# An mLSTM and Fourier-mixing kernel: its 64-row products cut into 64x64 tiles, and a one-column product widened to 128 columns

## The chip, the cores and the metric

The kernel runs on one core of one Trainium2 chip. Its time is the device time of one execution in microseconds (us), from start to end; less is better. A profile is one execution taken by the hardware profiler. It knows the engines PE (TensorE, matrix products), DVE (VectorE), ACT (ScalarE), POOL (GpSimd) and SP (which issues the DMAs here).

## The reference, cut to what matters

Two parts follow each other. The first is an mLSTM cell on q, k, v of shape (4 batches, 8 heads, 768 tokens, 40 features) with an input, a forget and an output gate. Step by step over the tokens it keeps a 40x40 state C and a vector n per head:

```
C = f * C + i * outer(v_t, k_t)      n = f * n + i * k_t
y_t = sigmoid(o_t) * (C q_t) / max(|n . q_t|, 1)      (f, i stabilised by a running maximum m)
```

The heads are joined to x of shape (4, 768, 320). The second part is a Fourier-mixing block:

```
u = x + real(fft(fft(x, axis=1), axis=2))
un = (u - mean(u)) / sqrt(var(u) + 1e-6)
out = u + relu(un @ w_ch1) @ w_ch2           (w_ch1 320x1280, w_ch2 1280x320)
```

All of it is in float32 (the two weight matrices come as float64 and are converted on the chip).

## The kernel before, in words

The mLSTM is worked in chunks of 128 tokens. In the first batch a chunk is a full 128x128 block of scores for each head (`mlstm_scores`, L591); in the three later batches it is two blocks of 64x64 (`halves_scores`, L678). Heads are packed in pairs: heads 0 to 3 lie on SBUF partitions 0 to 39, heads 4 to 7 on partitions 64 to 103, so one head's product has 40 rows and sits in the upper or lower half of the PE array. `product` (L580) is the helper that issues one matmul, and most of the small ones carry its line, L581. The pattern `TILES` (L653) runs through the four combinations of a row half and a column half of the array, in this order: (0,0), (1,1), (0,1), (1,0).

The Fourier transform along the tokens is a product with a table (`mix_products`, `mix_products_again`), and the one along the features is `mix_feat` (L961): for each of three groups of 128 frequencies, three matmuls into one PSUM bank `pu`. The 385th frequency (index `LAST` = 384) is left over. In the middle group two more matmuls have that one column of Z and Zt as the stationary operand and write one row of PSUM, `own`. `mix_add` (L983) reads that row.

The first matrix of the MLP has 320 input features: 128, 64 and 128. Full 128x128 matmuls (L1122, L1185) work the two blocks of 128 (in the later batches with a scheme that needs seven products for eight, whose sums DVE makes at L1194). The 64 features between are the "rest": `w1_rest(n)` holds 64 rows for an even block of hidden features on partitions 0 to 63 and 64 rows for the odd block on partitions 64 to 127. For these, two matmuls of 64 rows and 128 columns follow each other, one in the upper and one in the lower half of the array, each into its own PSUM bank of 128 hidden features by 384 tokens. In the first batch that is `between` (L1110, matmul at L1113), ten times; in each later batch it is `tails` (L1187, matmul at L1190), twice in step 2 of each of the five calls of `mlp_block`. There the order on PE is: a full product into bank p1, `tails(1)` into p3 and p5, `tails(0)` into p2 and p1, and in step 3 `begin(i + 1)`, a full product into the bank that p3 had. The matmul into p5 waits for a DVE sum (L1194), the one into p1 for an ACT copy (L1226), and `begin` for the DVE sum that reads p3. The second matrix (L1258 in the first batch, L1314 in the others) uses full tiles.

The order on each engine is written out by hand: `at(slot, phase, ...)` puts each function in a slot and `run` issues them slot by slot, so that pieces of one batch's mLSTM stand between pieces of the batch before's MLP. The four phases EVAC, FILL, MAIN and FILL_PE order the pieces within a slot. Every engine works its own list in that order and waits on semaphores.

A float32 matmul of the program shows in the trace as two weight loads (engine PEld) and two matmuls (engine PE), which I call its two passes; counts below are of these.

Of the kernel before, what the change touches and what calls it, by code (L numbers as in the profile page):

```python
# [19 lines left out]
L = 128  # L20
# [6 lines left out]
DM = H * D  # L27
DFF = 4 * DM
NFF = DFF // L
TAIL = DM - 2 * L  # L30
# [6 lines left out]
NC = HALF_D + 1  # L37
COL = (0, L, 2 * L)
LAST = 3 * L
# [18 lines left out]
def kernel(  # L58
# [15 lines left out]
    nc = tc.nc  # L74
# [15 lines left out]
    first_heads_ps = ps_early.enter_context(tc.tile_pool(name="ps_h", bufs=1, space=PSUM)).tile([L, 2, 4 * L], FP, name="hb")  # L90
# [3 lines left out]
    def bank(name, shape, n=None):  # L94

        return ps_m.tile(shape, FP, name=name, tag=f"pm{next(turn) if n is None else n}")
# [9 lines left out]
    dd_sb = const.tile([L, 4, DM + 1], FP, name="dd_sb")  # L106
# [20 lines left out]
    def at(slot, phase, fn, *args):  # L127
        plan.setdefault((slot, phase), []).append((fn, args))
# [16 lines left out]
    def gates(gp):  # L145
# [138 lines left out]
        pt = columns(first, 1)  # L284
        spread_max(0, 0, NP)
        mlstm_scores(0, 0)
        sums(others)
        mlstm_exp(0, 0, 0)
# [210 lines left out]
    def w1_block(ch, f):  # L499
        return w1_sb[:, f // 2, (2 * ch + f % 2) * L:(2 * ch + f % 2 + 1) * L]  # L500

    def w1_rest(n):
        return w1_sb[:, n, 4 * L:]
# [87 lines left out]
    def mlstm_scores(b, c):  # L591

        k = chunks[b, c]
        k.ps = [ps_s.tile([L, NP, L], FP, name=f"ps{hip}", tag="ps") for hip in range(2)]
        for p in range(NP):
            for hip in range(2):
                r = slice(hip * 64, hip * 64 + D)
                nc.tensor.matmul(k.ps[hip][:, p, :], k.qk[r, 1, p, :], k.qk[r, 0, p, :], start=True, stop=True)  # L598

    def mlstm_weigh(b, c):  # L600
        k = chunks[b, c]
# [49 lines left out]
    banks = {}  # L651

    TILES = ((0, 0), (1, 1), (0, 1), (1, 0))  # L653
# [8 lines left out]
    def half(n):  # L662
        return slice(n * LH, (n + 1) * LH)
# [297 lines left out]
    def mix_feat(b, p, part=slice(None)):  # L961

        k = mixes[b]
        m = slice(COL[p], COL[p] + L)
        if part.start in (None, 0):
            k.pu[p] = bank("pu", [L, DM + 1 + NC], MIX[b - 1]["u"][p] if b > 0 else None)
        pu = k.pu[p]  # L970
        if b == 0:
            products = ((pu[:, 0:DM + 1], k.Z[:, 0, m], dd_sb[:, 0]), (pu[:, 0:DM + 1], k.Z[:, 1, m], dd_sb[:, 1]),
                        (pu[:, 0:DM + 1], k.Zt[:, m], dd_sb[:, 2]))
        else:
            products = ((pu[:, 0:NC], k.Z[:, 0, m], dd_sb[:, 0, 0:NC]), (pu[:, NC:DM], k.Z[:, 1, m], dd_sb[:, 1, 1:HALF_D]),
                        (pu[:, 0:DM], k.Zt[:, m], dd_sb[:, 3, 0:DM]))
        if p == TG - 2:
            last, own = slice(LAST, LAST + 1), first_heads_ps[0:1, 1, 0:NC] if b == 0 else pu[0:1, DM + 1:]
            products += ((own, k.Z[:, 0, last], dd_sb[:, 0, 0:NC]), (own, k.Zt[:, last], dd_sb[:, 3, 0:NC]))
        for i, (o, z, t) in list(enumerate(products))[part]:  # L980
            nc.tensor.matmul(o, z, t, start=(i == 0 or b == 0 and i == 3), stop=(i in (2, 4)), skip_group_check=True)  # L981

# [74 lines left out]
    def plan_mix(b, s0, x_done, s_feat, s_add, s_turn):  # L1057
# [20 lines left out]
        for p in range(TG):  # L1078
            for i in range(3) if b == 0 and p == TG - 1 else ():
                at(s_feat[p] + i, FILL_PE + 5.1, mix_feat, b, p, slice(i, i + 1))  # L1080
            if b == 0 and p == TG - 2:
                at(s_feat[p], FILL_PE + 4.06, mix_feat, b, p, slice(0, 3))
                at(s_feat[p] + 3, FILL_PE + 5.05, mix_feat, b, p, slice(3, 5))
            elif b == 0 and p == 0:
                at(s_feat[p], FILL_PE + 4, mix_feat, b, p, slice(0, 2))
                at(s_feat[p], FILL_PE + 4.04, mix_feat, b, p, slice(2, 3))
            elif b > 0 or p < TG - 1:
                at(s_feat[p], FILL_PE + 4, mix_feat, b, p)
# [10 lines left out]
                at(t + 1, EVAC, mix_turn_out, b, c)  # L1099


    IN_ORDER = ((0, 0), (0, 1), (1, 0), (1, 1), (0, 2), (1, 2), (0, 3), (1, 3), (0, 4), (1, 4))

    def mlp_in(b, gr, f):


        k = mixes[b]
        u = [uT_bufs[gr][:, ch].rearrange("p c t -> p (c t)") for ch in range(3)]

        def between(pm, n, u, start):  # L1110
            for i in range(2):
                r = slice(i * TAIL, (i + 1) * TAIL)
                nc.tensor.matmul(pm[i], w1_rest(n)[r], u[r], start=start, stop=not start,  # L1113
                                 skip_group_check=True)


        n = IN_ORDER.index((gr, f // 2))
        ahead = n > 3 and n % 2 == 1
        if f % 2 == 0:
            k.pm = k.pm_next if ahead else [bank("pm", [L, TG * L]) for _ in range(2)]  # L1120
        for i, ch in ((1, 1),) if f % 2 else ((0, 0), (0, 1), (1, 0)):
            nc.tensor.matmul(k.pm[i], w1_block(ch, f // 2 * 2 + i), u[2 * ch], start=(ch == 0 and not ahead),  # L1122
                             stop=(ch == 1 and ahead), skip_group_check=True)
        if f % 2 and not ahead:
            between(k.pm, f // 2, u[1], False)
            if n > 3:
                k.pm_next = [bank("pm", [L, TG * L]) for _ in range(2)]
                gr, i = IN_ORDER[n + 1]
                between(k.pm_next, i, uT_bufs[gr][:, 1].rearrange("p c t -> p (c t)"), True)
# [4 lines left out]
    def hidden(gr, f):  # L1134
        return hid[gr, f % 2][:, f // 2 * TG * L:(f // 2 + 1) * TG * L]
# [7 lines left out]
    def block(t, n):  # L1143
        return t[:, n * L:(n + 1) * L]
# [20 lines left out]
    def mlp_u(gr, ch):  # L1165
        return uT_bufs[gr][:, ch].rearrange("p c t -> p (c t)")
# [8 lines left out]
    def mlp_block(b, i, step):  # L1175

        k = mixes[b]
        f = 2 * i  # L1180
        T2, T3, T4 = w1x["T"]
        A = {(r, ch): w1_block(ch, f + r) for r in range(2) for ch in range(2)}

        def product(bank, w, u, start=False):
            nc.tensor.matmul(bank, w, u, start=start, stop=True, skip_group_check=True)  # L1185

        def tails(gr, banks):  # L1187
            for r, bank in enumerate(banks):
                rows = slice(r * TAIL, (r + 1) * TAIL)
                nc.tensor.matmul(bank, w1_rest(i)[rows], mlp_u(gr, 1)[rows], start=False, stop=True,  # L1190
                                 skip_group_check=True)

        def add(h, bank):
            nc.vector.tensor_tensor(out=h, in0=h, in1=bank, op=OP.add)  # L1194

        banks = list(range(4) if i % 2 else range(3, -1, -1))

        def begin(i):


            k.p1 = bank("pm", [L, TG * L], 0 if i % 2 else 3)
            product(k.p1, w1_block(0, 2 * i), mlp_u(0, 0), True)
            nc.scalar.copy(out=hidden(0, 2 * i), in_=k.p1)

        (h11, h21), (h12, h22) = ([hidden(gr, f + r) for r in range(2)] for gr in range(2))
        if step == 0:
            if i == 0:
                begin(0)
            k.pm = [k.p1, bank("pm", [L, TG * L], banks[1])]
            product(k.pm[1], A[0, 1], mlp_u(0, 2), True)  # L1210
        elif step == 1:
            k.pm.append(bank("pm", [L, TG * L], banks[2]))
            p1, _, p5 = k.pm
            if i == 0:
                product(p5, A[1, 0], mlp_u(1, 0), True)
            product(p1, block(w1x["S2"], i), T2)
            nc.scalar.copy(out=h12, in_=p1)
            if i > 0:
                product(p5, A[1, 0], mlp_u(1, 0), True)
            add(h12, p5)  # L1220
        elif step == 2:
            k.pm.append(bank("pm", [L, TG * L], banks[3]))
            p1, p2, p5, p3 = k.pm
            product(p3, block(w1x["S4"], i), mlp_u(1, 2), True)
            product(p1, block(w1x["S3"], i), T3)
            nc.scalar.copy(out=h22, in_=p1)  # L1226
            tails(1, (p3, p5))
            tails(0, (p2, p1))
            add(h12, p3)
            add(h22, p5)  # L1230
            add(h11, p2)
        else:
            p1 = k.p1
            if i < NFF // 2 - 1:
                begin(i + 1)
            product(p1, A[1, 1], T4)
            nc.scalar.activation(out=h21, in_=p1, func=AF.Relu, scale=-1.0)
# [107 lines left out]
    def plan_mlp(b, s):  # L1345
        groups = range(NT // TG)
        for i in range(NFF // 2) if b > 0 else ():
# [4 lines left out]
            for n, (gr, f) in enumerate(((1, 2 * i + 1), (1, 2 * i), (0, 2 * i))):  # L1352
                at(*((s - 1, MAIN + (-0.1 if gr else 0.1)) if end else (s + n, MAIN + 0.5)), mlp_relu_in_place, gr, f)
        for gr, n in IN_ORDER if b == 0 else ():
            for f in (2 * n, 2 * n + 1):
# [248 lines left out]
```

## Time and profile before

| what | value |
|---|---|
| time, median of 3 runs | 397.08 us (395.04 to 399.1) |
| span of the profiled execution | 392.9 us |
| median of the runs over that span | 4.2 us |
| PE busy | 379.7 us, 97% of the span, 4342 matmuls |
| DVE, ACT, POOL busy | 281.2, 174.6, 134.9 us |
| granted PE clock | 1.000 |
| matmuls in tiles of 64 rows by 128 columns, busy | L1190 26.3 us (120), L1113 8.3 us (40), L598 7.0 us (96) |
| matmuls with one stationary column (L981), busy | 2.6 and 0.8 us (12 and 4) |

The profile gives the execution's span, from its first to its last instruction. Its own time with what lies around the span is not recorded; the median of the runs stands 4.2 us above it. Busy times of PE are not the work of the array: matmuls are pipelined and overlap, so the distance from one start to the next tells more than a duration. Rows written 64*128 mean 64 rows and 128 columns of the array in use; after that stand the partitions by elements of the moving operand.

### The profile page before, as it was taken

How to read it: one execution, taken by the hardware profiler on the slowest of the kernel's cores; microseconds unless marked ns; L12 is line 12 of the kernel's file. 1: busy time of each engine (PE TensorE's matmuls, PEld its weight loads, DVE VectorE, ACT ScalarE, POOL GpSimd, SP SyncE). 2: the span in 40 equal slices, each digit the busy share in tenths (PEclk: the TensorE clock that was granted, in tenths of full speed). 3: DMA queues.
4: the chain of work that ended last, by engine and by line, in shares of the span. 5: the costliest groups of instructions: out<-in, count | busy, mean ns of one | idle time of the engine just before them, and what ended most of it. 6: DMA issues, size and time to landing. Idle time of an engine off the chain costs nothing.

```text
span 392.9 us, 10881 instructions
## 1 busy us (share of the span) xinstructions
PE 379.7 (97%) x4342; PEld 277.5 (71%) x4342; DVE 281.2 (72%) x668; ACT 174.6 (44%) x505; POOL 134.9 (34%) x238
## 2 busy tenths in 40 slices
PE   8999888999999999999999998999999999999996
PEld 6888454556577767665478898666588996556996
DVE  7788898798897286787964796876855785346651
ACT  5978766757442133654443043654530033444000
POOL 5665434775595132561421424560300000020000
DMA  7869499697981343464002633710000001000000
GB/s 227 287 191 305 135 235 262 176 274 214 248 208 35 94 129 119 135 178 126 0 1 64 180 99 92 215 35 3 0 2 33 3 33 35 0 0 2 34 35 33
DMA packets 21614, 43.96 MB, mean 112 GB/s; under 512 B 3492, under 2 KB 9852, under 8 KB 21436
## 3 DMA queue, kind: packets, MB, share of 16 engines
q1 hardware_dynamic: 21564, 43.27, 37.5%
q8 instruction: 34, 0.56, 0.6%
q14 instruction: 16, 0.13, 0.1%
HBM read 39.16 MB, written 4.10 MB: 110 GB/s over the span
## 4 chain that ended last, share of the span: by engine, by line
PE 80%; DVE 11%; ACT 2%; issue 2%; DVEq 0%; ACTq 0%
PE po L1314 21%; PE pm L1185 16%; PE po L1258 8%; PE pm L1122 7%; PE pm L1190 6%; PE ph L581 5%; PE ps L581 4%; PE pu L981 3%; PE pz L936 2%; PE pm L1113 2%; PE hb L581 1%; PE put L1028 1%; PE pzt L936 1%; DVE so L771 1%; PE ps L598 1%
## 5 line engine op out<-in xcount | busy, mean ns | idle before, releaser
L1264 DVE SCALAR_TENSOR_TENSOR x<-po,rstd,x 128x160 f32<-128x160 f32 (+1 forms) x69 | 27.2, 394 | 38.8 <-PE po L1314 36.3
L1194 DVE TENSOR_TENSOR h<-h,pm 128x384 f32<-128x384 f32 x60 | 30.5, 548 | 26.8 <-PE pm L1190 12.4
L577 POOL TENSOR_SCALAR_AFFINE_SELECT W<-W 64x512 f32<-64x512 f32 x36 | 28.4, 790 | 32.5 <-ACT W L550 31.3
L704 POOL TENSOR_TENSOR C<-C,decB 128x164 f32<-128x164 f32 x33 | 19.1, 578 | 58.6 <-DVE C L711 52.5
L1185 PE MATMUL pm<-uT,w_sb 128*128 128x384 f32 x90 | 37.8, 507 | 0.2 <-DVE uT L1173 0.2
L550 ACT ACTIVATE W<-W,colT 128x64 f32<-128x64 f32 x144 | 36.6, 336 | 0.0
L1258 PE MATMUL po<-w_sb,h 128*128 128x320 f32 x120 | 34.1, 435 | 0.0
L1052 POOL TENSOR_TENSOR t<-rstd 128x6 f32<-128x6 f32 x12 | 3.7, 310 | 80.2 <-DVE v L1046 79.6
L562 POOL TENSOR_TENSOR qg<-qk,Gb 128x512 f32<-128x512 f32 x21 | 27.3, 1298 | 10.6 <-PE put L1028 10.3
L1122 PE MATMUL pm<-uT,w_sb 128*128 128x384 f32 x80 | 29.3, 499 | 0.7 <-issue 0.7
L1314 PE MATMUL po<-T,S 128*128 128x160 f32 x180 | 28.0, 302 | 1.1 <-DVE x L1264 1.1
L1258 PEld LDWEIGHTS po<-w_sb,h 128*128 128x128 f32 x120 | 22.3, 190 | 9.1 <-issue 0.6
L1314 PEld LDWEIGHTS po<-T,S 128*128 128x128 f32 x180 | 25.4, 190 | 2.7 <-DVE x L1264 1.3
L1190 PE MATMUL pm<-uT,w_sb 64*128 64x384 f32 x120 | 26.3, 511 | 0.3 <-DVE h L1194 0.3
L1314 PE MATMUL po<-w_sb,h 128*128 128x160 f32 x180 | 26.3, 300 | 0.0
L1314 PEld LDWEIGHTS po<-w_sb,h 128*128 128x128 f32 x180 | 25.2, 190 | 1.5 <-DVE x L1264 0.3
L1185 PEld LDWEIGHTS pm<-uT,w_sb 128*128 128x128 f32 x90 | 15.4, 189 | 13.9 <-DVE h L1194 5.9
L1241 ACT ACTIVATE h<-h 128x384 f32<-128x384 f32 x45 | 23.1, 519 | 3.0 <-DVE h L1194 3.0
L1017 ACT ACTIVATE uc<-x 128x384 f32<-128x384 f32 x24 | 14.4, 613 | 19.9 <-DVE x L1009 19.9
L1190 PEld LDWEIGHTS pm<-uT,w_sb 64*128 64x128 f32 x120 | 12.7, 185 | 12.8 <-issue 8.2
L1033 ACT COPY uT<-put 128x384 f32<-128x384 f32 x21 | 9.6, 477 | 26.9 <-PE put L1028 26.8
L1122 PEld LDWEIGHTS pm<-uT,w_sb 128*128 128x128 f32 x80 | 14.1, 189 | 10.4 <-issue 3.2
(259 smaller groups left out, 848.0 us busy)
## 6 DMA issues: line engine op xcount, KB each, us to landing
kvt<-in_kv SPq DMA_DIRECT2D x24, 336.0 KB
qk<-in_qkT SPq DMA_DIRECT2D x48, 160.0 KB
raw<-in_w SPq DMA_DIRECT2D x10, 640.0 KB
Gb<-G_d SPq DMA_DIRECT2D x42, 128.0 KB
W<-M_d SPq DMA_DIRECT2D x36, 128.0 KB
so<-in_o SPq DMA_DIRECT2D x24, 160.0 KB
out<-x SPq DMA_DIRECT2D x24, 160.0 KB
ds_sb<-in_dft_s SPq DMA_DIRECT2D x1, 1158.0 KB
```

The costliest lines, as they stand in the source:

```text
L550: nc.scalar.activation(out=k.W[:, h, :], in_=M, func=AF.Exp, scale=-1.0, bias=colT[:, c, 0, b * H + h:b * H + h + 1])
L562: nc.gpsimd.tensor_tensor(out=k.qg[:, :, t], in0=k.qk[:, 0, :, t], in1=k.Gb[:, :, t], op=OP.mult)
L577: nc.gpsimd.affine_select(out=W, in_=W, compare_op=OP.is_ge, fill=0.0, base=base, pattern=[[0, H], [-1 if back else 1, LH]], channel_multi ...
L581: nc.tensor.matmul(out, w, x, start=start, stop=True, skip_group_check=True)
L1122: nc.tensor.matmul(k.pm[i], w1_block(ch, f // 2 * 2 + i), u[2 * ch], start=(ch == 0 and not ahead), stop=(ch == 1 and ahead), skip_group_c ...
L1185: nc.tensor.matmul(bank, w, u, start=start, stop=True, skip_group_check=True)
L1190: nc.tensor.matmul(bank, w1_rest(i)[rows], mlp_u(gr, 1)[rows], start=False, stop=True, skip_group_check=True)
L1194: nc.vector.tensor_tensor(out=h, in0=h, in1=bank, op=OP.add)
L1241: nc.scalar.activation(out=h, in_=h, func=AF.Relu, scale=-1.0)
L1258: nc.tensor.matmul(k.po[m], hidden(gr, f)[:, i * L:(i + 1) * L], w2_sb[:, f, :], start=(f == 0), stop=(f == NFF - 1))
L1264: nc.vector.scalar_tensor_tensor(out=u, in0=po, scalar=k.rstd[:, c:c + 1], in1=u, op0=OP.mult, op1=OP.add)
L1314: nc.tensor.matmul(po, a[:, f], w[:, f], start=start and f == 0, stop=f == half - 1, skip_group_check=True)
```

## The change

Three places change, all in the order and form of matmuls; no other engine's instructions do.

1. `rest_products` takes the place of the two matmuls of `between` and of `tails`. Each matmul of 64 rows by 128 columns becomes two of 64 by 64 (column half 0, then column half 1), so a pair becomes four: upper and lower half for the first 64 hidden features, then upper and lower half for the other 64. The moving operand, 384 tokens, is the same for both column halves.
2. `mlstm_scores` of the first batch does the same with its 40 rows by 128 columns: each matmul becomes two with 64 keys, in the order of `TILES`.
3. In `mix_feat` the stationary column of the last frequency is repeated 128 times (a broadcast view, no copy), and `own` is 128 equal rows of PSUM in place of one. `mix_add` still reads row 0.

```
-            for hip in range(2):
+            for hip, i in TILES:
                 r = slice(hip * 64, hip * 64 + D)
-                nc.tensor.matmul(k.ps[hip][:, p, :], k.qk[r, 1, p, :], k.qk[r, 0, p, :], start=True, stop=True)
+                product(k.ps[hip][half(i), p, :], k.qk[r, 1, p, half(i)], k.qk[r, 0, p, :], True)
...
-            last, own = slice(LAST, LAST + 1), first_heads_ps[0:1, 1, 0:NC] if b == 0 else pu[0:1, DM + 1:]
-            products += ((own, k.Z[:, 0, last], dd_sb[:, 0, 0:NC]), (own, k.Zt[:, last], dd_sb[:, 3, 0:NC]))
+            own = first_heads_ps[:, 1, 0:NC] if b == 0 else pu[:, DM + 1:]
+            z, zt = (t[:, LAST:LAST + 1].to_broadcast([L, L]) for t in (k.Z[:, 0], k.Zt))
+            products += ((own, z, dd_sb[:, 0, 0:NC]), (own, zt, dd_sb[:, 3, 0:NC]))
...
+    def rest_products(banks, n, u, start):
+        for cols in range(2):
+            for i in range(2):
+                nc.tensor.matmul(banks[i][half(cols)], w1_rest(n)[half(i), half(cols)], u[half(i)], start=start,
+                                 stop=not start, skip_group_check=True)
...
         def between(pm, n, u, start):
-            for i in range(2):
-                r = slice(i * TAIL, (i + 1) * TAIL)
-                nc.tensor.matmul(pm[i], w1_rest(n)[r], u[r], start=start, stop=not start,
-                                 skip_group_check=True)
+            rest_products(pm, n, u, start)
...
         def tails(gr, banks):
-            for r, bank in enumerate(banks):
-                rows = slice(r * TAIL, (r + 1) * TAIL)
-                nc.tensor.matmul(bank, w1_rest(i)[rows], mlp_u(gr, 1)[rows], start=False, stop=True,
-                                 skip_group_check=True)
+            rest_products(banks, i, mlp_u(gr, 1), False)
```

## The prediction

> **What bounds the kernel now.** I read the page's busy times and chain first, then the chain of waits in order of time, window by window, then the timeline around single groups.
>
> ```profile
> PE 379.7 (97%) x4342; PEld 277.5 (71%) x4342; DVE 281.2 (72%) x668; ACT 174.6 (44%) x505; POOL 134.9 (34%) x238
> ...
> PE 80%; DVE 11%; ACT 2%; issue 2%; DVEq 0%; ACTq 0%
> ```
>
> PE is the bound, but not everywhere: the chain lies on DVE and ACT from 31.3 to 61.6 us and at 170.6 to 181.1, 227.9 to 237.1 and 266.3 to 269.0. Time saved on PE counts where the chain is on PE, or where DVE was itself waiting for PE. In the chain of waits (start, duration, what, count) three stretches hold the prices:
>
> ```profile
> 19.38 0.60 PE hb L581 x16
> 19.98 1.09 PE ps L598 x16
> 21.07 1.02 PE hb L581 x16
> ...
> 87.95 0.61 PE ph L581 x32
> 88.55 0.80 PE ps L581 x64
> 89.36 0.47 PE ph L581 x32
> 89.82 3.42 PE pm L1122 x10
> 93.25 1.49 PE pm L1113 x8
> 94.73 0.61 PE ph L581 x32
> ...
> 136.79 1.28 PE pu L981 x6
> 138.07 2.69 PE po L1258 x10
> 140.76 1.72 PE pu L981 x10
> 142.48 2.89 PE po L1258 x10
> ```
>
> What is to be seen: a group costs more when the group before it had another tile shape. 32 matmuls in 64x64 tiles take 0.61 us after a change of shape and 0.47 later within one shape: 0.14 for the change. Fourteen full matmuls at L1185 take 4.71 us (194.46 in the same chain), ten at L1122 take 3.42, so one is (4.71 - 3.42) / 4 = 0.32, and 4.71 - 14 x 0.32 leaves 0.20 for the change. The eight of L1113 run two at a time: four steps of 0.32 are 1.29, and 0.20 is left again. **So the change of shape costs 0.20 us into 128 columns and 0.14 into 64.** The first load cannot be fetched ahead there; L1190's loads take 185 ns on average and those of L581's `ps<-qk` 134, which gives the same 0.05.
>
> **The MLP's rest, part by part.** A pair of 64x128 matmuls already fills the array. Four 64x64 tiles do the same work in the same two steps of 0.32 us, so "four at a time" saves nothing in the steps. It saves at the edges: 0.05 at each entry from full tiles, and the whole entry of 0.14 where L581's 64x64 work stands right behind (94.73 above), as no change of shape is left. The exit to full tiles stays at 0.20. Where these lie in the chain:
> - First batch: seven entries, three of them followed by L581 (63.7, 78.3, 94.7): 7 x 0.05 + 3 x 0.14 = 0.77. All on PE's chain.
> - Second batch, five blocks: 165.3, 185.5 and 199.2 give 0.05 each, 0.15. Those at 174.3 (with L581 behind it) and 191.7 give nothing, below.
> - Third: 253.8, 262.9, 273.4 and 286.2 give 0.20, and L581 behind the second 0.14; 279.6 nothing: 0.34.
> - Fourth: five of 0.05, 0.25. Here each block is 1.49 and 4.78 with nothing else in it, so this stage shows the price most purely.
>
> ```profile
> 174.72 0.66 DVE fe L874
> ...
> 177.18 0.65 DVE h L1194 x2
> ...
> 191.78 0.49 ACT h L1226
> 192.27 0.03 issue
> 192.30 0.56 DVE h L1194
> 192.86 0.04 issue
> 192.90 1.55 PE pm L1190 x6
> ```
>
> At 174 DVE works through its own list (181.1 is when PE gets its next release), so an earlier PE gains nothing. At 191.7 and 279.6 the matmul into p5 waits for DVE's sum. There the new order has a price: the second column halves of p3 and p5 stand behind that wait, where before p3 ran ahead alone. p3 is then done with p5, two steps (0.64) later than now, and DVE's sum of p3 (0.55), which `begin` needs, ends about as late as PE's last tile. I take the 0.05 for lost and the bound at -0.1 each. The wait of p1 for ACT's copy (166.67) holds up p2's second half the same way, but both are wanted only after p1, and ACT was released by PE.
>
> **The last frequency.** The six matmuls of a group take 1.28 - 0.20 = 1.08 us without the entry. In 140.76 the same six and four more take 1.72: 0.64 for the four. They stream 161 columns like two of the six, 0.134 each, 0.54, so 0.10 is the change into one column; the 2.89 behind it against the usual 2.69 is the change back, 0.20. With 128 columns both go and the load of 190 ns lies beside the matmul before. 0.30 a batch; at 142, 222 and 308 it counts (0.90), at 57 it doesn't: DVE is at its own work until 59.0.
>
> **The first batch's scores.** From 1.09 us: the 64x64 group ahead of it takes 0.60 for 16, minus 0.14 is 0.11 to 0.12 for four matmuls of 128 columns. Eight such steps are 0.9, with no entry since shape and neighbour agree: 0.19 less. Chunks 2, 3 and 4 lie on the chain, 0.57; the other three save 0.05 off it. Behind them the chain goes through ACT (31.33 on) and DVE, fed by DMAs with a busy share of 0.76 before 31 us. Nothing shows what comes next there: bounds 0 and 0.57; I take 0.40, since ACT and DVE are released by PE at the seam.
>
> **Waits added.** As built, the new program holds 23 waits of PE on its own earlier matmuls, on a bank that 64x64 tiles wrote last. The nearest target is 38 matmuls back, microseconds earlier, so the wait itself is over. Seven are instructions of their own on PE's list; such ones take 51 ns today, beside running matmuls. 0, at most 7 x 0.05 = 0.35. All other engines keep order and waits; SP's and POOL's queues are passed by nothing. PE's list grows by 256 matmuls and 256 loads. PE once stops for 0.73 us at 81.82 with no cause shown; if that is the list's supply, it may move: 0.7 either way.
>
> **Sum.** 0.77 + 0.15 + 0.34 + 0.25 + 0.90 + 0.40 = 2.8 us: the span goes from 392.9 to 390.1. With the 4.2 around it, or from the median of 397.08, **394.3 us**, 0.7% less. The runs shown differ by 1%, so within 1% is about what a measurement here can't tell from no change.
>
> **Rivals.**
> - *Everything counts* (0.14). With the edges that I gave up, 0.57 - 0.40, 0.30 at 57, 0.14 and 3 x 0.05 in the DVE stretches, it is 3.6 us: 393.5. For it: DVE partly waits for PE even there.
> - *Others take over* (0.12). If DVE, ACT and DMAs hold the old pace up to 269 us, only 308, 286 and the fourth batch are left and one block of the third, 0.65: 396.4. For it: DVE's stretches above; against: each begins at a release by PE.
> - *Loads of one row half exclude its matmuls* (0.08). Two column tiles now share each row half. If the load for the second pass had to wait for matmuls in the same half, each step after a set's first would show its load: 45 steps in L1190 and 13 in L1113, 58 x 0.05 = 2.9, which eats the gain: 397.2; with whole loads of 134 ns 58 x 0.13 = 7.5, 401.8. Against it, the 64x64 groups of today load while they run:
>
> ```profile
> 24.06 0.51 PE L581 MATMUL hb<-qg,C 40*64 40x128 f32 x12
> ...
> 24.07 0.26 PEld L581 LDWEIGHTS hb<-qg,C 40*64 40x64 f32 x8
> ```
>
> [...]
> - *Slower: the four tiles don't stream together* (0.04). If one row half can feed only one column half its 384 moving columns at a time, each of 40 sets takes 0.64 more, 25.7, and 48 score steps 0.11 more: about 425. It decides from the first set, at 62.8 us. Against it: 16 matmuls of 128 columns in 0.60. For it: those have 40 rows, not 64, and the two column tiles read different columns.
>
> **How the numbers follow.** The forecast has 0.62. The range goes from the full gain, less some 1.2 for the spread of the runs, 392.2, to the mild case of the third rival, 397.2. Faster by over 1% (below 393.1): half of the first rival and a fifth of the forecast, by the spread, 0.20. Slower by over 1%: the last rival and the dear end of the third, 0.07. Within 1%: 0.73.
>
> **What will show it.** In the fourth batch 1.49 should become 1.44 beside an unchanged 4.78; ten matmuls at L981 about 1.6 and the next group 2.69; L581 behind the rest 0.47 in place of 0.61; scores 0.9. A set near 2.7 would mean the last rival, 1.6 or more the third. I am wrong if these come and the end doesn't move: then DVE or DMAs took it.

## The result and the profile after

The changed kernel takes 393.95 us (median of 20 runs, 391.01 to 397.99), the kernel before 396.47 us on the same chip (20 runs, 394.55 to 401.45). The ratio is 0.994 with a 95% interval of 0.991 to 0.997: 2.4 us less, where 2.8 were forecast. The span of the profiled execution went from 392.9 to 391.3 us. Executions more than 1.5% above the fastest of their kernel are left out of all ratios, though not of the medians; the profile of one experiment below (part 1 alone) is such an execution, so only its pause and its clock are read from it.

The page of the changed kernel: busy times, the queue that brings instructions (packets, MB, share), and the shares of the chain.

```profile
PE 378.4 (97%) x4598; PEld 275.4 (70%) x4598; DVE 282.4 (72%) x668; ACT 175.3 (45%) x505; POOL 134.1 (34%) x238
...
q8 instruction: 36, 0.59, 0.6%
...
PE 83%; DVE 8%; issue 2%; ACT 1%; DMA 1%; POOL 0%; SPq 0%; DVEq 0%; ACTq 0%
```

PE has 256 matmuls more and 1.3 us less of busy time. Its instructions come in 36 packets instead of 34; that is taken up below.

The chain of waits of the changed kernel (start, duration, what, count), at the places that the prediction named:

```profile
19.91 0.60 PE hb L581 x16
20.51 0.87 PE ps L581 x32
...
89.22 3.42 PE pm L1128 x10
92.65 1.45 PE pm L1108 x16
94.10 0.45 PE ph L581 x32
...
139.91 1.63 PE pu L982 x10
141.54 2.69 PE po L1261 x10
...
192.13 1.51 PE pm L1108 x14
...
193.65 4.78 PE pm L1191 x14
...
219.72 1.63 PE pu L982 x10
221.35 5.66 PE po L1317 x40
...
331.42 1.45 PE pm L1108 x16
332.87 0.01 issue
332.88 4.78 PE pm L1191 x14
```

Nearly every price came as forecast. Scores take 0.87 us (forecast 0.9, before 1.09). A set of the first batch takes 1.45 (1.49 before), and the L581 group behind it 0.45 in place of 0.61: its change of shape is gone. Ten matmuls of the last frequency take 1.63 (1.72 before), and the group behind them 2.69 (2.89). In the third batch, though, the group behind is 5.66 us, where it was 5.64 with the change of shape in it: there the exit's 0.20 came back as something else. And in the block at 192.13 the loss that the prediction described is there: 1.51 and 4.78, together as long as before.

### The profile page after: what moved, and what is told of

The parts are those of the page before. It is cut to its first block, busy times and chain, and to the rows that moved or that the text cites. A ratio compares the mean times of both kernels' runs of the same rounds, so it can differ in the third digit from the quotient of the medians.

```text
span 391.3 us, 11400 instructions
## 1 busy us (share of the span) xinstructions
PE 378.4 (97%) x4598; PEld 275.4 (70%) x4598; DVE 282.4 (72%) x668; ACT 175.3 (45%) x505; POOL 134.1 (34%) x238
## 4 chain that ended last, share of the span: by engine, by line
PE 83%; DVE 8%; issue 2%; ACT 1%; DMA 1%; POOL 0%; SPq 0%; DVEq 0%; ACTq 0%
PE po L1317 21%; PE pm L1191 17%; PE po L1261 8%; PE pm L1108 8%; PE pm L1128 7%; PE ph L581 5%; PE ps L581 4%; PE pu L982 3%; PE pz L936 2%; PE hb L581 1%; PE put L1029 1%; PE pzt L936 1%; PE pz L948 1%; DVE so L771 1%; DVE stats L1009 1%
## 5 line engine op out<-in xcount | busy, mean ns | idle before, releaser
L550 ACT ACTIVATE W<-W,colT 128x64 f32<-128x64 f32 x144 | 36.8, 338 | 0.0
L1108 PE MATMUL pm<-uT,w_sb 64*64 64x384 f32 x320 | 34.1, 498 | 0.4 <-DVE h L1197 0.4
L1191 PEld LDWEIGHTS pm<-uT,w_sb 128*128 128x128 f32 x90 | 15.4, 189 | 14.7 <-DVE h L1197 6.7
L1108 PEld LDWEIGHTS pm<-uT,w_sb 64*64 64x64 f32 x320 | 11.5, 131 | 20.3 <-issue 16.2
L568 POOL TENSOR_TENSOR vw<-kvt,colT 128x328 f32<-128x328 f32 x23 | 20.1, 875 | 4.8 <-DVE colT L289 2.5
```

Of the source, the lines that this page charges most:

```text
L550: nc.scalar.activation(out=k.W[:, h, :], in_=M, func=AF.Exp, scale=-1.0, bias=colT[:, c, 0, b * H + h:b * H + h + 1])
L1108: nc.tensor.matmul(banks[i][half(cols)], w1_rest(n)[half(i), half(cols)], u[half(i)], start=start, stop=not start, skip_group_check=True)
```

## The experiments

### Each part alone

Part 1 alone has the new `rest_products` and the old scores and last frequency; part 3 alone and part 2 alone are the other two hunks of the diff. Parts 1 and 3 ran on one chip, part 2 on another.

> Only the MLP's rest in 64x64 tiles; scores and last frequency as before. My theory (the gain lies at the edges of a set, where the tile shape changes): in the fourth batch a set takes 1.45 us in place of 1.49 and a block 6.25 in place of 6.27; behind a set in the first batch L581 takes 0.14 less; L981's ten matmuls stay at 1.72 and the group behind them at 2.89. Span from the first 128x128 transposes of the chain (L1028, near 62 us) to the end: 0.8 to 1.2 us shorter, ratio 0.997. Rival (the gain that the changed kernel showed between 62 and 110 us is the pause of 0.73 us at 81.8 that happened not to come): the stretch from there to the first products at L1258 is shorter by under 0.3 us wherever the pause is there, and the ratio is 1.000.

> Only the last frequency's stationary column repeated to 128; the rest as before. My theory: the ten matmuls at L981 take 1.63 us in place of 1.72 and the group behind them 0.20 less, in each of the three later batches, 0.29 each; what of it is left at the end depends on who waits next. In the changed kernel 0.38 was lost again at 151 us and 0.2 at 224; if DVE's own pace takes it, both losses come again here (0.3 to 0.5 us left of 0.87, ratio 0.999). Rival (the loss at 151 us is a pause that comes by chance): nothing is lost at 151, only at 224; 0.6 to 0.7 us left, ratio 0.998.

> Part 2 alone: only the first batch's scores are cut into 64x64 tiles. The predicted theory: each of the six groups of scores goes from 1.09 to about 0.87 us, and 0.40 of the 0.57 us of the groups on the chain reach the end: ratio 0.999. Rival: ACT, DVE and the DMAs take the whole of it back before 62 us (in the changed kernel the chain at 62 us was already 0.42 us late): the first product into the MLP's first bank starts at 61.6 us or later, and the ratio is 1.000. Both lie inside the interval of the times, so the trace decides: 61.2 us for that start by the first theory, 61.6 or later by the second.

| kernel | median us (runs) | kernel before, same chip | ratio, 95% interval |
|---|---|---|---|
| part 1, rest | 393.25 (13) | 394.97 | 0.9938 (0.9909 to 0.9968) |
| part 2, scores | 394.38 (12) | 396.39 | 0.9946 (0.9911 to 0.9982) |
| part 3, last frequency | 396.07 (12) | 394.97 | 1.000 (0.9975 to 1.0026) |

The three gains do not add up: 0.6 and 0.5 and 0 per cent make 1.1, and together they are 0.6; with intervals of about 0.3 each side this alone could be noise. But they go against the traces too. Part 3 shows its 0.30 at 140.5 and 305.6 us in its own trace, as forecast, and none of it in the time. Here the granted clock of PE, which is recorded for every execution, matters: ten of part 3's twelve executions had a mean clock below 0.998. The two at full clock have a median of 393.63 us, against 394.62 for the fourteen such executions of the kernel before. For part 1 it is 393.00 (5), for part 2 393.05 (2) against 395.04 (11). "Why PE pauses" returns to this. Part 2 shows nothing in the trace that could be 2 us. Its chain in the first batch:

```profile
19.69 0.87 PE ps L581 x32
...
28.55 2.70 DMA so<-in_o
31.25 1.27 POOL qg L562
32.57 1.69 PE hb L581 x32
...
41.33 1.92 PE pz L948 x4
...
47.39 1.50 PE pz L948 x4
```

The scores are 0.22 us shorter, but then the chain leaves PE for a DMA that lands at 31.25 and POOL's work on it, where it was on PE and ACT before. The first group of the MLP (L1028) starts at 61.36 us against 61.63, and the whole stretch was already 0.28 us early at 17 us, ahead of any edited group. So in this trace nothing of the scores' gain reaches the MLP, as the second theory of that expectation says. But the two traces did not have the same clock. Here it is halved from 41.9 to 45.3 us, and PE is on the chain there (four matmuls at L948 take 1.92 us, four later ones 1.50); in the trace of before it is not. From the start of the pG group ahead of them to the MLP's first group (L1028 here), the five traces with the old scores and no such dip before 62 us take 43.98 to 44.41 us, the two with the new scores 43.80 and 44.56. What the scores are worth at the end stays open. What else differs between this trace and the one of before is a pause of PE: 0.73 us at 81.82 us before, gone here. It is taken up below.

### Two more changes of shape in each block

To price the edges in the fourth batch, the product with T4 is moved between the two `tails` of a block, in the old and in the new form. Each block then has two sets apart, so one more entry and one more exit.

```
             tails(1, (p3, p5))
+            product(p1, A[1, 1], T4)
             tails(0, (p2, p1))
...
-            product(p1, A[1, 1], T4)
             nc.scalar.activation(out=h21, in_=p1, func=AF.Relu, scale=-1.0)
```

> The kernel before, with one change: in mlp_block the last full product into p1 stands between the two sets (upper and lower halves of the second group, then of the first), so that each of the 15 blocks has one change of tile shape more in each direction; all matmuls are the same. My theory: 0.20 into 64x128 and 0.20 out of it, 0.40 a block, less the 0.06 that the next block's first product now waits for DVE's sum: 6.27 becomes 6.61 in the fourth batch; in all 13 to 15 blocks 4.5 to 5.5 us longer, ratio 1.012 to 1.014. Rival (the edges cost nothing of their own, the matmuls' distance is set by something else): a block stays at 6.27, ratio 1.000.

> The changed kernel with the same reordering as the split of the kernel before. My theory: an extra entry into 64x64 costs 0.14 to 0.15 and the exit 0.20, 0.35 a block less the 0.06 of DVE's wait: 6.25 becomes 6.53 in the fourth batch; 3.5 to 4.5 us longer than the changed kernel, that is 1.5 to 2 us longer than before, ratio to before 1.004 to 1.006, and 0.05 a block less than the other split. Rival (a set of 64x64 tiles has another gain than its entry): the distance between the two splits is that between the unsplit kernels, 0.025 a block and not twice the entry's 0.05.

Measured: 404.39 us, ratio 1.0216 (1.0163 to 1.027), with the old tiles, and 401.39 us, 1.0138 (1.0091 to 1.0185), with the new ones. The chain of waits in the fourth batch, first with 64x128 tiles, then with 64x64:

```profile
338.93 0.84 PE pm L1190 x4
339.77 0.84 PE pm L1185 x2
340.61 0.84 PE pm L1190 x4
341.46 4.26 PE pm L1185 x12
```

```profile
338.14 0.81 PE pm L1108 x8
338.94 0.84 PE pm L1191 x2
339.79 0.81 PE pm L1108 x8
340.59 4.26 PE pm L1191 x12
```

Two steps of 0.32 are 0.645, so an entry or an exit costs 0.195 each with 128 columns, and the new entry is 0.03 to 0.04 cheaper, near the 0.05 of the prediction. The block went from 6.27 to 6.79 us, though, 0.52 and not 0.34 more; fifteen blocks of 0.52 are 7.8 of the 9.4 us by which the first median lies above the kernel before, where 4.5 to 5.5 were expected. The 4.26 us hold 12 x 0.3225 = 3.87, the exit's 0.195, and 0.195 that are new. The timeline of the first kernel shows them:

```profile
342.34 0.48 ACT L1203 COPY h<-pm 128x384 f32<-128x384 f32 x1 [2.90 <-PE pm L1185]
...
342.87 0.30 PEld L1185 LDWEIGHTS pm<-raw 128*128 128x128 f32 x2 [0.54 <-ACT h L1203]
```

With the T4 product gone from between, only two matmuls cover ACT's copy of p1, and the next product into p1 waits for it: 0.09 us of wait, and 0.10 because the load of the waiting matmul is no longer beside another's stream (both begin at 342.87 us). The two moved matmuls had hidden that.

Old and new tiles are 0.08 us apart in these blocks (6.79 and 6.71), but only 0.02 in the blocks as they are (6.27 and 6.25). The timeline of one set of the changed kernel tells why:

```profile
331.35 1.52 PE L1108 MATMUL pm<-uT,w_sb 64*64 64x384 f32 x16
...
331.72 0.47 PEld L1108 LDWEIGHTS pm<-uT,w_sb 64*64 64x64 f32 x8 [0.17 <-issue]
332.27 1.48 DVE L1197 TENSOR_TENSOR h<-h,pm 128x384 f32<-128x384 f32 x3 [1.23 <-PE pm L1108]
332.88 0.30 PEld L1191 LDWEIGHTS pm<-uT,w_sb 128*128 128x128 f32 x2 [0.68 <-DVE h L1197]
```

`begin`, the first full product behind the set, waits for DVE's sum of p3, which ends 0.055 us before it starts: also in the kernel before, and in every block of this stage. The time from the set's first matmul to `begin` is set by p3's end and DVE's 0.555 us, not by the exit, so of 0.04 saved about half is left. In the split blocks the second set's exit is followed by a product that no sum holds up.

The same lines decide the rival of the exclusive loads. The loads for the later passes run from 331.72 on beside matmuls in the same two row halves, and the steps behind a set's first stay at 0.32 us, so none of them shows a load.

### The order of rows and columns

```
-        for cols in range(2):
-            for i in range(2):
+        for i in range(2):
+            for cols in range(2):
```

> The changed kernel with the two loops of the rest exchanged: both column halves of the upper row half, then both of the lower. Theory: at 191.7 and 279.6 us the second column half of p3 stood behind the wait of p5 for DVE's sum, and begin for DVE's sum of p3. With p3 complete ahead of the wait, that sum starts about 0.5 us earlier, begin is held by PE alone, and each of the two blocks gains 0.05 to 0.15 us; the blocks without a late sum change by less than 0.03. Together 0.1 to 0.3 us, below what the times can show. Rival: begin is held there by the four tiles themselves, and the two blocks stay at 1.51 us.

In the block at 191.7 the set itself stays at 1.51 us, but there and in the one at 279.6 the full products behind it take 4.71 in place of 4.78: `begin` no longer waits for DVE, since p3 is complete before the matmul that waits. That is 0.07 us a block, within the expected 0.05 to 0.15. The time of the one execution (396.07 us, span 394.4) says nothing on that. PE's granted clock was halved for about 3 us, and here it fell on the chain; in the windows of PE, PEld, DVE, ACT and POOL the clock is the third number from the end:

```profile
66.00:68.00 2.00, 2.00 (x70) 1.92 (x63) 1.82 (x2) 0.65 (x2) 1.94 (x2) 0.50 1.02 317
```

The changed kernel's own profile has such a dip too (its mean clock is 0.996), at 40.8 to 44.2 us. PE is on its chain there: four matmuls at L948 take 2.16 us at 42.62, and 1.50 at 47.94.

### Putting 64x64 groups side by side

If the gain is the change of shape, more of it is to be had by letting more groups of the mLSTM stand right behind a set. For the third and fourth batch's mLSTM the stride of its slots is four, as that of the MLP's blocks, in place of three. The slots of `mix_fold_again` and of what follows the mLSTM move with it.

```
-            at(s + 3, MAIN - 0.1 if end else FILL_PE, halves_from_state, b, c)
+            at(s + stride, MAIN - 0.1 if early_end else FILL_PE, halves_from_state, b, c)
...
-            plan_halves(b, s_mlstm)
+            plan_halves(b, s_mlstm, 3 if b == 1 else 4)
...
-    plan_batch(2, 54, 83, s_mlp + 2 * MLP_SLOTS)
-    plan_batch(3, 86, 115, s_mlp + 3 * MLP_SLOTS)
+    plan_batch(2, 53, 83, s_mlp + 2 * MLP_SLOTS)
+    plan_batch(3, 85, 115, s_mlp + 3 * MLP_SLOTS)
```

> The changed kernel with the mLSTM of the third and the fourth batch put on a stride of four slots in place of three, so that each of its groups of 64x64 products stands right behind a set of the rest. If the price of a change of tile shape (0.14 us into 64 columns, 0.20 back) is what the change saves, four isolated groups in each of two batches lose their pair of changes: 8 x 0.34 = 2.7 us less than the changed kernel, a ratio of about 0.987 to the kernel before. Rival: the order of DVE's work decides there (the chain lies on DVE at 171 to 181 and 258 to 269 us), and the moved mLSTM brings its sums late at other places: ratio 0.994 as the changed kernel, or worse.

> The kernel before with the same new order. The groups stand behind a set there too, but the set has 64x128 tiles, so a change into 64 columns (0.14 us) stays at each: 8 x 0.34 - 8 x 0.14 less what the one neighbour in each batch paid already, 1.9 us less than the kernel before, a ratio of 0.995; the distance to the same order with 64x64 tiles should be about 3.2 us, where it was 2.4 in the old order. Rival: if the order acts through DVE alone, both orders have the same distance of 2.4 us.

Slower, both: 401.72 us with the new tiles, ratio 1.0101 (1.0058 to 1.0144), and 400.24 with the old ones, 1.0127 (1.0056 to 1.0198). The chain of the first shows the gain and what ate it:

```profile
163.20 1.45 PE pm L1109 x16
164.65 0.45 PE ph L581 x32
...
168.28 0.52 ACT h L1245
168.79 1.91 ACT W L550 x8
170.70 0.37 ACT h L1221
```

The group behind the set costs 0.45, without its change. But ACT's eight exponentials of the next chunk (L550, 1.91 us) now stand ahead of ACT's copy of p1 (L1221) in the same slot, and the next product into p1 waits for that copy: PE works on other products meanwhile and stands idle for the last 0.68 us before 171.11. That happens in two blocks of each of the two batches, 2.7 us of idle time in all. Three more waits are for DVE's `uT` (L1180), 2.7 us with 1.9 the longest; the changed kernel has one, of 0.2. The old tiles in the new order have the same waits. So the rival held, with ACT beside DVE.

Whether the tiles still make a difference in this order the medians can't tell, as the clocks differ. In the new tiles' trace it is halved from 251.9 to 255.3 us, and six products there take 3.87 us where the other trace, at full clock, has 2.37:

```profile
251.77 3.87 PE pm L1192 x6
```

```profile
253.60 2.37 PE pm L1186 x6
```

The executions at full clock have medians of 397.69 us with the new tiles (2) and 400.14 with the old (3). That is 2.45 less: nearer to the rival's 2.4 than to the 3.2 expected, from very few executions.

### Why PE pauses

A pause of PE that the chain calls "issue" had been left open by the prediction. The traces of the first ten kernels held eight pauses of over 0.9 us (from one start on PE to the next) with no wait that the profile shows. They have one thing in common. If the matmuls, weight loads and stand-alone waits of PE are counted from the beginning of the trace, PE stops at entry 193 + 256 n and nowhere else. A packet of the instruction queue brings about as many, as an estimate from the kernel before: 34 packets of 16 KB for 8770 entries, 258 each.

| kernel | pause, us | ends at, us | entry | = 193 + 256 x | from the start of packet n to the end of the pause, us |
|---|---|---|---|---|---|
| before | 1.22 | 82.55 | 1985 | 7 | 2.76 |
| part 3 alone | 1.13 | 82.28 | 1985 | 7 | 2.51 |
| split, old tiles | 1.31 | 83.28 | 1985 | 7 | 2.61 |
| new order, old tiles | 1.49 | 82.74 | 1985 | 7 | 2.94 |
| split, new tiles | 1.68 | 86.34 | 2241 | 8 | 2.84 |
| part 1 alone | 1.98 | 179.39 | 5057 | 19 | 2.54 |
| new order, new tiles | 0.95 | 185.94 | 5313 | 20 | 2.48 |
| new order, new tiles | 1.92 | 260.46 | 7105 | 27 | 2.61 |
| changed kernel (a smaller one) | 0.52 | 150.97 | 4289 | 16 | 2.72 |

About 0.32 of each is the normal step. I read this as PE running out of instructions: the packet with its next 256 has begun to move, and PE goes on 2.5 to 2.9 us after that. A group of the mLSTM (32, 64 and 32 matmuls with as many loads in 1.9 us) uses up a whole packet in less time than that, and where PE stopped, a mark had fallen into or just behind such a group. The packets begin about when PE enters the packet before (between 5.1 us ahead and 4.4 us behind in all traces, 0.9 behind in the middle). PE ran dry with one packet outstanding: in the kernel before that packet began at 79.79 us, PE went on at 82.55, and the next packet began only at 84.41.

Marks move with the number of entries ahead of them. That is a thing to test: small matmuls without any use, put where PE waits for ACT (60.3 to 61.6 us), move all marks behind. They also keep PE busy where it had waited.

```
             pt = k.pt[c] = banks["heads"][:, n % 2, 0:3 * L].rearrange("p (ch t) -> p ch t", ch=3)
+            for m in range(10 if n == TG else 0):
+                i, j = TILES[m % 4]
+                product(banks["heads"][half(j), i ^ j, 4 * L - 4:4 * L], ident[half(i), half(i)], ident[half(i), 0:4], True)
```

Each such matmul is four entries; 10, 28, 10 and 24 of them are used.

> The kernel before with ten small extra matmuls (40 entries of PE's list, 64x64 tiles, four columns) put where PE waits for ACT at 60.3 to 61.6 us; their result is read by nobody. Theory of the list: PE's instructions come in packets of 256 (16 KB, 34 of them), PE stops at entry 193 + 256 n of its list if it gets there less than about 2.6 us after packet n began to move, and a packet begins about 0.6 us (quiet DMAs) to 1.4 us (busy) after PE passed entry 193 + 256 (n - 1). Forty entries more move these marks into the dense 64x64 groups: pauses of about 2.0 us (1.0 to 2.6) near 80.2 us and 2.0 us near 149.5 us in place of the 0.9 us at 81.8: 3.2 us longer (2.2 to 4.4), ratio 1.008. Rival: the pauses have another cause, and the extra matmuls fall into PE's idle time: ratio 1.000, the pause where it was.

> The same with 28 extra matmuls (112 entries). Theory of the list: the marks fall into full-tile work nearly everywhere, the pause at 81.8 goes and none comes in its place: 0.8 us shorter, less at most 0.3 us for the extra matmuls if they do not fit into PE's idle time, ratio 0.998. Rival: as the kernel before, the pause at 81.8 stays, or all is longer by the extra matmuls. The trace decides, as the times show 0.8 us hardly.

> The changed kernel with ten extra matmuls (40 entries) in the same place. Theory of the list: pauses near 80.3 and 148.8 us (2.0 us each) and near 228 and 249 us (1.4 each, the one at 228 beside a stretch where the chain lies on DVE) in place of 0.4 at 84 and 0.2 at 151: 4 to 6 us longer than the changed kernel, a ratio of 1.004 to 1.009 to the kernel before, so that the whole gain is lost. Rival: as the changed kernel, 0.994.

> The changed kernel with 24 extra matmuls (96 entries) in the same place. Theory of the list: no mark falls into a dense group, so the pauses of 0.4 us at 84 and 0.2 us at 151 go, and none comes: 0 to 0.6 us shorter than the changed kernel, a ratio of 0.992 to 0.994 to the kernel before, and 6 us shorter than the same kernel with 40 entries. Rival: no difference between 40 and 96 entries beyond the 0.3 us that the extra matmuls may take.

All four on one chip, where the kernel before took 397.64 us (29 runs, 394.1 to 402.07):

| kernel | median us (runs) | lowest to highest | ratio to before, 95% interval | profiled execution, us | pauses over 0.9 us |
|---|---|---|---|---|---|
| before + 40 entries | 394.07 (12) | 393.22 to 397.76 | 0.994 (0.9905 to 0.9975) | 394.04 | none |
| before + 112 | 393.89 (12) | 393.18 to 395.71 | 0.9939 (0.9903 to 0.9975) | 393.72 | 1.43 at 177.46, entry 5057 |
| changed + 40 | 396.63 (12) | 393.5 to 400.36 | 0.9987 (0.9944 to 1.003) | 393.57 | 2.39 at 79.28, entry 2241 |
| changed + 96 | 392.08 (6) | 391.6 to 393.23 | 0.9892 (0.9842 to 0.9942) | 392.45 | none |

The two new pauses lie on marks again (n = 19 and 8), 2.71 and 2.48 us after their packets began; with these, ten pauses of over 0.9 us in 14 traces, all on marks, and none of 476 marks was passed less than 2.33 us after its packet began. The changed kernel with 40 entries has the expected pause at 80 us, in the chain:

```profile
79.05 0.45 PE ph L581 x31
79.50 2.17 issue
81.67 0.25 PE ph L581
```

**By the medians, ten useless matmuls make the kernel before 0.6% faster**, as much as the whole change. The theory of the list holds in what it says of the place of a pause and of its end. It failed in where I expected pauses: with 40 entries the old kernel should have had two of 2.0 us, and has none, the changed kernel four, and has one; with 112 there should have been none, and there is one. So the expected time failed too: a ratio of 1.008 with 40 entries, and 0.994 came. I had let a packet begin after PE passed the mark before it. But where full tiles stand ahead of a dense group, PE works few entries in a long time, and in this kernel the packet began 2.74 us ahead of the mark at 78.65 us. When exactly a packet is asked for stays open.

How can a pause of 0.73 us in the chain be worth 3.6 us of the median? The spread of the executions goes with PE's granted clock. Of the executions that count for the ratios on this chip, these are the medians in us (and their number), by the mean clock of the execution:

| kernel | clock 0.998 or more | lower |
|---|---|---|
| before | 394.49 (8) | 397.93 (18) |
| before + 40 entries | 394.03 (7) | 394.33 (5) |
| before + 112 | 393.73 (10) | 395.34 (2) |
| changed + 40 | 393.54 (3) | 396.92 (8) |
| changed + 96 | 391.83 (2) | 392.28 (4) |

At full clock the useless matmuls are worth 0.46 and 0.76 us, about the one pause that goes. The rest of the 3.6 us is that fewer executions ran at a lower clock, and less slowly. A dip in the traces is a clock of 0.50 for 3.4 us, or twice that, so one of 3.4 us can take 1.7 us at most. The changed kernel's trace, with one such dip, has a mean clock of 0.996, and 15 of the 18 executions of the kernel before in the right column lie at 0.994 to 0.996: where 3.4 us are between the columns, something else comes with the dip. Pauses may bring dips: in part 1 alone a dip of 6.8 us, on the chain, begins 1.3 us after the end of the pause at 179.39 us. But the longest pause, 2.39 us in the changed kernel with 40 entries, has no dip behind it, and no execution of the kernel before with a lower clock was profiled. So what lowers the clock stays open, and with it the part of the marks in the timed difference: the extra matmuls may also act by keeping PE busy at 60 us.

The profiled execution's own time is its span plus 1.7 to 1.8 us in the changed kernel and in ten of the experiments (2.1 and 2.3 in the two with the new order). The kernel before, by its span 394.65, has medians of 394.97 to 397.64 in the four sets of runs beside the other kernels: its profile, at a clock of 1.000, is one of its executions at full clock. Only one execution of each kernel was profiled, so the size of the pauses in the timed runs is not shown.

With this a fair comparison is possible: old tiles with 40 entries and new tiles with 96, both without such a pause, on one chip: 394.07 and 392.08 us, 1.99 less, ratio 0.995 (0.993 to 0.997, by resampling the runs); at full clock it is 2.2 less. And stage by stage, from the chains of the kernel before with 40 entries and of the changed one with 96:

```profile
62.04 0.55 PE ph L1031 x3
...
109.69 10.96 PE po L1261 x40
...
288.01 2.72 PE po L1317 x20
...
359.72 29.31 PE po L1317 x210
```

```profile
62.20 0.55 PE ph L1032 x3
...
109.14 10.96 PE po L1264 x40
...
286.79 2.72 PE po L1320 x20
...
358.10 29.33 PE po L1320 x210
```

The new kernel is 0.16 us late at 62 and 1.62 early at 359. Of the 0.16, 0.11 were there at 17 us, ahead of any edit, and only the new kernel's trace has a clock dip (41.2 to 44.6 us). The changed kernel with 96 entries, at 0.989, is also the fastest version found, ahead of both kernels.

## Why the prediction was right, and where it was not

The forecast, 394.3 us, stands 0.35 beside the measured 393.95, and the change is within 1%, the likeliest of the three classes. That it is so near is in part luck: the median of three runs that it started from, 397.08, was 0.61 above that of the later twenty, and the terms of the sum, 2.8 us, show only 1.6 in the traces where 2.4 were timed. Term by term, from the pair without pauses:

| term | forecast us | measured us |
|---|---|---|
| first batch's rest | 0.77 | 0.71 |
| last frequency, second batch (142) | 0.30 | 0.26 |
| second batch's rest | 0.15 | 0.06 |
| last frequency, third batch (222) | 0.30 | 0.09 |
| third batch's rest | 0.34 | 0.26 |
| last frequency, fourth batch (308) | 0.30 | 0.28 |
| fourth batch's rest | 0.25 | 0.12 |
| first batch's scores | 0.40 | not resolved (-0.16 at 62 us, with the clock dip) |
| sum | 2.8 | 1.6 |

**The mechanism was right.** What the change saves is changes of tile shape, 0.20 into 128 columns, 0.14 into 64 and 0.20 out, and a whole 0.14 where an L581 group follows. In the trace of the kernel before, a load between full tiles starts with the matmul ahead of its own (92.44 us both), the first load of the set at 93.17 only with its own. Four tiles work at the step of a pair, 0.32 us. Of waits of PE on itself the changed kernel's trace shows one, 0.20 us at 151.08, where mark 4289 lies too. The two rivals on loads and on tiles that do not stream together fell with the first set. That everything counts fell with the terms that come next; that others take over held at these places only.

**Cover was missed in two terms.** The fourth batch was to show the price "most purely", with "nothing else in it". In fact `begin` waits for DVE's sum in each of its blocks, so half of the step saved is handed back (the set's timeline above). At 222 us the exit's 0.20 was counted, and the group behind it met a bank that DVE was still adding from; the timeline of the changed kernel has that wait on the load of the third ten matmuls of the group:

```profile
223.57 0.38 DVE L1267 SCALAR_TENSOR_TENSOR x<-po,rstd,x 128x160 f32<-128x160 f32 x1
...
224.00 1.38 PEld L1317 LDWEIGHTS po<-T,S 128*128 128x128 f32 x10 [0.18 <-DVE x L1267]
```

The step that failed is the 0.20 of the change back, "the 2.89 behind it against the usual 2.69", counted at 142, 222 and 308: it was read off one of three places and carried to the others; the third batch's row (5.64 for 40) was not looked at for what stands behind it. The second and the third batch's rest lack 0.09 and 0.08; that is about the 0.07 that the wait of `begin` costs in each of the blocks at 191.7 and 279.6, by the order of rows and columns; the prediction had bounded it at 0.1 and put it at nothing. For the scores I chose 0.40 between 0 and 0.57 because ACT and DVE are released by PE there. The chain then went through a DMA's landing and POOL, a path that the prediction did not have; what is left of the 0.57 behind it stays open.

**The list may have covered the misses.** Of the measured 2.4 us, 1.6 (by the trace) to 2.0 (by the times) are the edges. What is left, 0.4 to 0.8, lies within the interval of the 2.4 (1.3 to 3.4), so it need not be anything. The list is one candidate: the change put 519 entries more into it and so moved its marks away from the dense group at 82 us. In the chain there were 0.73 there before; after, the set at 83.37 takes 1.85 us in place of 1.45, with mark 2241 in it, and 0.18 stand at 150.9. That the marks moved and that pauses stand on them is shown; how much of the timed difference they are, and how much the clock is, is not. The prediction had the possibility, "if that is the list's supply, it may move: 0.7 either way", and gave it no place in the sum. It was the same size as the errors, with the other sign. With another number of entries the same change measured next to nothing: with 40 more it is at 0.9987 (0.9944 to 1.003), though at full clock these executions too are 0.95 us below the kernel before (393.54 and 394.49).

**The 4.2 us around the span were no constant.** They were 1.75 around it and 2.4 by which the median of three runs was slower than the profiled one. For the changed kernel the two are 1.75 and 0.9. Taking the forecast span of 390.1 with the right 1.75 would have given 391.9, near the changed kernel without pauses; the sum of 4.2 carried the old kernel's slower executions over into the forecast.

## What to carry to other kernels

Price a tile's shape by its neighbours: what was saved here is not work but the change between shapes, 0.34 us a pair, and it counted only where nothing else, a sum on another engine, ended at the same time. Before such small gains are measured, compare executions at the same granted clock, as those at a lower one were up to 3.4 us longer here. Then look at PE's list: where many small matmuls stand together, count its entries and look for pauses without a releaser at an equal distance, 256 entries here; the marks move with every instruction that is added or taken away ahead of them, and a version with a few idle matmuls in PE's waiting time tells how far a difference of half a per cent hangs on more than the change.

## What was not expected of the hardware

- PE paused for over 0.9 us without a wait that the profile shows only at entries 193 + 256 n of its list, ten times in 14 traces, for up to 2.39 us; it went on 2.5 to 2.9 us after packet n began to move.
- Ten matmuls without use, in a waiting time of PE, moved the median from 397.64 to 394.07 us and the highest run from 402.07 to 397.76; at full clock only from 394.49 to 394.03.
- PE's granted clock was 0.50 for 3.4 or 6.8 us in some executions (the last microseconds apart): at about 41 to 47 us in seven of the 14 traces, and at 65, 181 and 252 us in one each, where it lay on the chain.
- The time from the beginning to 17 us, ahead of any edit, differs between executions: the pG group ahead of the first scores starts at 16.90 to 19.18 us.
